# PReLU feed-forward over linear attention: four feature tiles of the first product by seven quarter products, and a computed order of loops 2 to 8

## The chip, the cores and the metric

The kernel runs on one core of a Trainium2 chip. The metric is the time of one execution on the device in microseconds (us), lower is better; runs of the unchanged kernel took 273.03, 273.45 and 273.68 us. The core has TensorE (PE, matmuls into PSUM), VectorE (DVE), ScalarE (ACT), GpSimd (POOL, here mostly for issuing DMAs) and SyncE (SP, for issuing DMAs). Each engine works through its own list of instructions in order, and semaphores tie the lists together.

## The reference

```
kv  = einsum('bhsd,bhse->bhde', k, v)           # batch 8, heads 8, seq 576, head_dim 64
o   = einsum('bhsd,bhde->bhse', q, kv)
o   = o / sqrt(mean(o*o, axis=-1) + 1e-6) * g_norm
x   = o.transpose(0,2,1,3).reshape(4608, 512)
h   = x @ w_in                                  # 512 -> 2048, the first product
g   = maximum(h, 0) + alpha * minimum(h, 0)
out = g @ w_out                                 # 2048 -> 512, the second product
```

## The kernel before

Matmul operands are float16, sums are float32 in PSUM. The 4608 tokens are cut into nine blocks of 512 (w = 0 to 8). x of a block lies transposed (feature rows, tokens along the free axis) in xt, two blocks at a time. The first product makes a block of h in sixteen tiles of 128 features by 512 tokens: m1_mm (L600) is four matmuls of 512 columns into one PSUM bank. m1_neg (L609, ScalarE) writes relu(-h) into m_sb, and m1_sum (L615, VectorE) makes g = h + (1 - alpha) * relu(-h) in float16 into gt.

The second product is already done with seven instead of eight products of quarters, from block 1 on (prod_mm, L796): a block of g is cut into halves of tokens and of features, w_out likewise; w_sum prepares sums of weight quarters once, s_sum (L731 to L737, VectorE) sums of g quarters, sixteen per block. Products 1 and 2 gather in PSUM bank X, 6, 7 and 4 in bank Y, 5 and 3 in bank Z, which is the same bank as Y. y_read takes the sums out: p1 and c11 by ScalarE copies (L824, L834), u2, u3, c21, c22, c12 by VectorE adds (L828, L838, L840) to parts read earlier. c11, c21, c22 are stored by GpSimd's queue and c12 by SP's.

Attention of block w + 1 runs inside loop w: row_kv (L1122) makes k'v of one batch, ScalarE copies it masked into kv_masked (L1134); rows_mm (L499) makes attention rows of two 128-token tiles at a time; rows_sq, rows_rs and rows_norm (L556 to L580) square, sum, take the reciprocal root and scale. A tile is squared either in eight 64-wide squares with an accumulator (L562) or, where 'red' is set, in one square and a VectorE reduction (L558); 'red' is set for one of four tiles in a steady loop. SP transposes the rows into xt (L585) and q into qt_sb (L380). Loads of k, v, q go out on GpSimd behind a small copy that waits for a given gt (gate), into two stage tiles per name (kst, vst, qst), two blocks ahead.

The order is written out by hand. Block 0 and the set-up stand before the loops; in loop w (1 to 8) each of sixteen units u emits one tile of the first product, then the sums listed for u (S_ALL, S_ONE, S_TWO, S_LST), then as many products of the second product as the lists X_AT and YZ_AT say (X of this block and Y, Z of the block before), then steps of attention (ROW_AT), transposes and loads. From block 2 on the tiles of the first product take turns in two PSUM banks (h1, h2), Y and Z in h0, X in a bank of its own, and attention has two pairs of banks (psr). After loop 8 the rest of block 8's second product follows.

## Time and profile before

| what | us |
|---|---|
| median of the runs | 273.45 (273.03 to 273.68) |
| span of the profiled execution, first to last instruction | 271.4 |
| median less that span | 2.05 |
| steady loop (block 3 to block 4, start of L631 to start of L631) | 27.59 |
| PE, DVE, ACT, POOL busy in that loop | 27.59, 23.27, 17.11, 11.33 |
| last loop; from its last tile to the end | 24.86; 13.86 |

The profile is of one execution; its own time beyond the span is not recorded apart, so the median of the runs stands beside it. A group's row gives the kernel's line, engine, operation, tile written and read, the shape, the count, the busy time with the mean of one, and the idle time ahead of it with what ended it. In a timeline a row gives the start, the time to the end of the last instruction merged into it, and the count. Durations of neighbours on an engine overlap, so the cost of one in a stream is the distance from its start to the next start.

### The profile page before, as it was taken

The page shows a single profiled execution, that of the slowest core. Times are in us where ns is not written, and L with a number is a line of the kernel's source. Part 1 is how long each engine was busy: PE and PEld are TensorE (multiplying, and loading weights), DVE is VectorE, ACT ScalarE, POOL GpSimd, SP SyncE. Part 2 cuts the span into 40 slices and gives each one's busy share as a digit, 9 for nine tenths or more (in the row PEclk, how much of TensorE's full clock was granted, in tenths as well). Part 3 has the DMA queues.
Part 4 walks back from the last instruction along what each step waited for, and adds up shares of the span by engine and source line. Part 5 has one row for each costly group of instructions (what it writes and reads, how often), then busy time and mean ns, then how long its engine had stood idle before and what let it go on. Part 6 is the DMA issues. An engine that isn't in the chain of part 4 may idle for free.

```text
span 271.4 us, 6175 instructions
## 1 busy us (share of the span) xinstructions
PE 265.4 (98%) x2286; PEld 168.8 (62%) x2286; DVE 216.9 (80%) x413; ACT 156.7 (58%) x532; POOL 87.5 (32%) x134
## 2 busy tenths in 40 slices
PE   7899999999999999999999999999999999999995
PEld 3354444456666666667666666666666666766684
DVE  6459657998959986998699869986998889878964
ACT  3467575786559447754776467546855864433410
POOL 8763462514551735163515351430110011101100
PEclk9999999999999999999999999999999999999999
DMA  7999999995999999969995999594061122211123
GB/s 155 195 202 203 195 198 194 160 212 101 157 129 243 159 165 140 170 105 177 135 159 105 174 121 156 131 151 102 19 138 40 41 47 88 62 40 40 40 77 118
DMA packets 91570, 35.58 MB, mean 131 GB/s; under 512 B 62980, under 2 KB 89748, under 8 KB 91540
## 3 DMA queue, kind: packets, MB, share of 16 engines
q0 software_dynamic: 57872, 23.83, 69.8%
q1 hardware_dynamic: 32628, 10.34, 22.8%
q10 hardware_dynamic: 1040, 1.02, 1.2%
q8 instruction: 18, 0.29, 0.4%
q14 instruction: 12, 0.10, 0.2%
HBM read 36.71 MB, written 9.44 MB: 170 GB/s over the span
## 4 chain that ended last, share of the span: by engine, by line
PE 81%; DMA 15%; POOL 2%; issue 1%; DVE 0%; POOLq 0%
PE h_ps L600 37%; PE yY L796 16%; PE yX L796 10%; PE yZ L796 10%; DMA w_out_sb<-in_moe_w_out_dram 5%; DMA vst<-in_v_dram 4%; DMA w_in_sb<-in_moe_w_in_dram 3%; DMA qst<-in_q_dram 2%; PE h_ps L631 2%; PE kv_ps L1122 2%; PE or_ps L499 2%; PE y L643 1%; PE yZ L791 1%; POOL w_in_sb L229 1%; PE kv_ps L418 0%
## 5 line engine op out<-in xcount | busy, mean ns | idle before, releaser
L600 PE MATMUL h_ps<-xt,w_in_sb 128*128 128x512 f16 x540 | 136.1, 379 | 0.0
L609 ACT ACTIVATE m_sb<-h_ps 128x512 f32<-128x512 f32 x144 | 86.6, 602 | 79.4 <-PE h_ps L600 59.9
L615 DVE SCALAR_TENSOR_TENSOR gt<-m_sb,beta_sb,h_ps 128x512 f16<-128x512 f32 x144 | 106.1, 743 | 23.1 <-ACT m_sb L609 20.5
L600 PEld LDWEIGHTS <-w_in_sb 128*128 128x128 f16 x540 | 51.4, 98 | 39.7 <-issue 0.4
L655 POOL DMA_DIRECT2D out_dram<-y_sb x32 | 20.5, 645 | 119.6 <-DVE y_sb L838 56.9
L796 PEld LDWEIGHTS <-s 128*128 128x128 f16 x496 | 48.3, 98 | 11.3 <-DVE s L733 0.3
L796 PEld LDWEIGHTS <-gt 128*128 128x128 f16 x384 | 37.5, 98 | 23.2 <-issue 0.2
L796 PE MATMUL yX<-w_out_sb,gt 128*128 128x256 f16 x256 | 44.6, 273 | 0.0
L796 PE MATMUL yY<-wsum,s 128*128 128x256 f16 x256 | 35.2, 273 | 0.0
L562 ACT ACTIVATE sq_sb<-or_ps 128x64 f16<-128x64 f32 x144 | 30.9, 256 | 2.3 <-PE or_ps L499 2.3
L562 ACT ACTIVATION_READ_ACCUMULATOR sq_sb<-or_ps 128x1 f32 x144 | 30.3, 242 | 0.0
L580 DVE TENSOR_TENSOR x_rows<-or_ps,rstd_r 128x512 f16<-128x512 f32 x27 | 18.4, 686 | 1.0 <-ACT rstd_r L572 1.0
L185 POOL DMA_DIRECT2D qst<-in_q_dram x20 | 17.7, 905 | 1.0 <-issue 1.0
L828 DVE TENSOR_TENSOR u<-yY,p 128x512 f32<-128x512 f32 x16 | 11.0, 690 | 8.2 <-PE yY L796 8.2
L796 PE MATMUL yY<-wsum,gt 128*128 128x256 f16 x128 | 17.6, 272 | 0.0
L796 PE MATMUL yZ<-wsum,s 128*128 128x256 f16 x120 | 17.5, 273 | 0.0
L796 PE MATMUL yZ<-w_out_sb,s 128*128 128x256 f16 x120 | 16.7, 273 | 0.0
L643 PE MATMUL y<-w_out_sb,gt 128*128 128x512 f16 x64 | 16.3, 379 | 0.3 <-DMA w_out_sb<-in_moe_w_out_dram 0.3
L731 DVE TENSOR_TENSOR s<-gt 128x512 f16<-128x512 f16 x32 | 13.3, 420 | 0.1
L733 DVE TENSOR_TENSOR s<-s,gt 128x512 f16<-128x512 f16 x32 | 12.8, 421 | 0.4
L737 DVE TENSOR_TENSOR s<-gt,s 128x512 f16<-128x512 f16 x32 | 12.7, 419 | 0.0
L735 DVE TENSOR_TENSOR s<-gt 128x512 f16<-128x512 f16 x32 | 12.3, 419 | 0.0
(107 smaller groups left out, 233.2 us busy)
## 6 DMA issues: line engine op xcount, KB each, us to landing
out_dram<-y_sb POOLq DMA_DIRECT2D x16, 256.0 KB, 2.8
kst<-in_k_dram POOLq DMA_DIRECT2D x7, 512.0 KB, 7.3
vst<-in_v_dram POOLq DMA_DIRECT2D x6, 512.0 KB, 8.0
qst<-in_q_dram POOLq DMA_DIRECT2D x20, 128.0 KB, 4.7
w_out_sb<-in_moe_w_out_dram POOLq DMA_DIRECT2D x8, 256.0 KB, 11.0
out_dram<-y_sb SPq DMA_DIRECT2D x5, 256.0 KB, 2.2
w_in_sb<-in_moe_w_in_dram POOLq DMA_DIRECT2D x2, 512.0 KB, 10.2
qst<-in_q_dram POOLq DMA_DIRECT2D x2, 512.0 KB, 12.1
```

The costliest lines, as they stand in the source:

```text
L185: nc.gpsimd.dma_start(out=st[:, t, :, :], in_=srcs["q"][b, :, t * P : (t + 1) * P, :].rearrange("h p d -> p h d"),)
L562: nc.scalar.activation(out=sq[:, half, j], in_=o_ps[:, half, j], func=AF.Square, accum_out=ssq[:, half, j : j + 1],)
L580: nc.vector.tensor_tensor(out=xr[:].rearrange("p j h d -> p h j d"), in0=o_ps, in1=rstd[:].unsqueeze(3).to_broadcast([P, 2, NPAIR, D]), op ...
L600: nc.tensor.matmul(out=h_ps[:], lhsT=w_in_blk(c, g), rhs=xts[w][:, c, :], start=(c == 0), stop=(c == NC - 1),)
L609: nc.scalar.activation(out=neg[w, g][:], in_=h_ps[:], func=AF.Relu, scale=-1.0)
L615: nc.vector.scalar_tensor_tensor(out=gts[w, i][:, r, :], in0=neg.pop((w, g))[:], scalar=beta_sb[:, g : g + 1], in1=h_ps[:], op0=ALU.mult, ...
L643: nc.tensor.matmul(out=y[:], lhsT=gt_cols(w, g, a * P, (a + 1) * P), rhs=w_out_blk(g), start=(n == 1), stop=(n == NF),)
L655: engs[store_turn[0] % len(engs)].dma_start(out=dst, in_=src)
L731: nc.vector.tensor_add(out=t[:], in0=a21, in1=a22)
L733: nc.vector.tensor_sub(out=t[:], in0=sums[w, 1, k][:], in1=a11)
L737: nc.vector.tensor_sub(out=t[:], in0=a12, in1=sums[w, 2, k][:])
L796: nc.tensor.matmul(out=bank, lhsT=lhs, rhs=rhs, start=fresh, stop=(c == NK - 1), skip_group_check=True,)
```

## The change

From block 3 on, the first product is done in two of its four feature groups (s = 2 and 3) by seven quarter products. A group is four feature tiles, 2s, 2s + 1 and 2s + 8, 2s + 9; its weights are cut into halves of features and of the contraction, x into halves of the contraction and of tokens. a_sum prepares four sums of weight quarters per group once, in stage tiles that are no longer used for loads; x_sum prepares four sums of x quarters per block. Products 1, 6, 7, 4 gather in one bank (Y) with ScalarE copies in between, the copy 'seed' also starts bank X for product 2, and 5 and 3 gather in bank V with VectorE adding u3 and u2 (c22, c12). Relu and PReLU sum follow per half, 256 wide, or, where 'asm' is set, 512 wide after one more copy.

In the second product bank Y is filled with p1 by a copy before product 6 (y_seed), so that u2, u3 and c21 are plain ScalarE copies. The feature order of all loops is F_ORDER, and the feature halves of the second product are LO and HI. From block 3 on k, v, q have one stage tile each. m_sb has four buffers in place of two, the first product four banks (h1, h2, m0, m1) in place of two, attention one pair of banks in place of two. In blocks 3 to 8 two tiles of a block are squared with the reduction in place of one, and one is normalised on ScalarE in eight pieces.

Loops 2 to 8 are no longer written out: each piece of work is a task with an engine, a cost in us, a due time and its dependencies; run_plan goes through time and gives each free engine the ready task that is due first; the instructions are emitted in that order.

```diff
+    M_BUFS = 4
...
+    def late_pools():
+        mid.close()
+        row_pool[:] = [
+            ctx.enter_context(tc.tile_pool(name="psr2", bufs=1, space=bass.MemoryType.PSUM))
+        ]
+        m_pool.append(
+            ctx.enter_context(tc.tile_pool(name="psm", bufs=1, space=bass.MemoryType.PSUM))
+        )
...
+    def stage_for(b, nm, shape):
+        if b < B_NAT:
+            return stage_tile(nm, shape)
+        if nm not in kept:
+            kept[nm] = stage_tile(nm, shape)
+        return kept[nm]
...
+    LO = (0, 4, 1, 5)
+    HI = (2, 6, 3, 7)
+    F_ORDER = [f for s in range(4) for f in (2 * s, 2 * s + 1, 2 * s + 8, 2 * s + 9)]
...
+    def s_sum(w, n, k, pool=0):
+        lo, hi = gts[w, LO[k]], gts[w, LO[k] if n == 3 else HI[k]]
...
+    def y_seed(w):
+        ybank[w, "Y"] = ps_h.tile([P, 2, HC], FP32, name="yY", tag="h0")
+        nc.scalar.copy(out=ybank[w, "Y"][:], in_=part[w, 1][:])
...
     def y_read(w, what, subs=(0, 1)):
+        seeded = 1 <= w < NW - 1
         if what == "p1":
             part[w, 1] = u_p.tile([P, 2, HC], FP32, name="p1")
             nc.scalar.copy(out=part[w, 1][:], in_=ybank[w, "X"][:])
             return
         if what in ("u2", "u3"):
             part[w, what] = u_p.tile([P, 2, HC], FP32, name=what)
+            if seeded:
+                nc.scalar.copy(out=part[w, what][:], in_=ybank[w, "Y"][:])
+                return
             nc.vector.tensor_add(
                 out=part[w, what][:], in0=ybank[w, "Y"][:], in1=part[w, 1][:]
             )
             return
         y_sb = ysb_p.tile([P, 2, HC], FP32, name="y_sb")
-        if what == "c11":
-            nc.scalar.copy(out=y_sb[:], in_=ybank[w, "X"][:])
+        if what == "c11" or what == "c21" and seeded:
+            nc.scalar.copy(out=y_sb[:], in_=ybank[w, what == "c11" and "X" or "Y"][:])
...
-    w_sum(3, 0)
+    w_sum(4, 1)
+    w_sum(3, 1)
...
+    M1_FROM = {2: 3, 3: 3}
...
+    def a_sum(s, n, pool=0):
+        if s not in spare:
+            spare[s] = stage_tile(SPARE[s], [P, 4, HD, 2 * P])
+        t = spare[s]
+        eng = nc.gpsimd if pool else nc.vector
+        sub, add = eng.tensor_sub, eng.tensor_add
+        if n == 1:
+            add(out=t[:, 0], in0=w_quad(1, s, 0), in1=w_quad(1, s, 1))
+        elif n == 2:
+            sub(out=t[:, 1], in0=t[:, 0], in1=w_quad(0, s, 0))
+        elif n == 3:
+            sub(out=t[:, 2], in0=w_quad(0, s, 0), in1=w_quad(1, s, 0))
+        else:
...
+    def x_sum(w, n, pool=0):
+        t = sum_p.tile([P, HD, HW], FP16, name=f"t{n}", tag=f"t{n}", bufs=1)
+        xsums[w, n] = t
+        sub = (nc.gpsimd if pool else nc.vector).tensor_sub
+        if n == 1:
+            sub(out=t[:], in0=x_quad(w, 0, 1), in1=x_quad(w, 0, 0))
+        elif n == 2:
+            sub(out=t[:], in0=x_quad(w, 1, 1), in1=xsums[w, 1][:])
+        elif n == 3:
+            sub(out=t[:], in0=x_quad(w, 1, 1), in1=x_quad(w, 0, 1))
+        else:
+            sub(out=t[:], in0=x_quad(w, 1, 0), in1=xsums[w, 2][:])
...
+    def m1_prod(w, s, n, bank, fresh):
+        t = m1s[w, s]
+        quad = {1: (0, s, 0), 2: (0, s, 1), 4: (1, s, 1)}.get(n)
+        lhs = w_quad(*quad) if quad else spare[s][:, {5: 0, 6: 1, 7: 2, 3: 3}[n]]
+        rhs = {1: (0, 0), 2: (1, 0), 3: (1, 1)}.get(n)
+        rhs = x_quad(w, *rhs) if rhs else xsums[w, {4: 4, 5: 1, 6: 2, 7: 3}[n]][:]
+        for c in range(HD):
+            for r in range(2):
+                nc.tensor.matmul(
+                    out=t[bank][:, r, :], lhsT=lhs[:, c, r * P : (r + 1) * P], rhs=rhs[:, c, :],
+                    start=(fresh and c == r == 0), stop=(c == HD - 1), skip_group_check=True,
+                )
+
+    def m1_fast(w, s, n, tags):
+        t = m1s.setdefault((w, s), {})
+        bank = {1: "Y", 6: "Y", 7: "Y", 4: "Y", 2: "X", 5: "V", 3: "V"}[n]
+        if n in (1, 5):
+            t[bank] = m1_bank(tags[bank], [P, 2, HW], f"m{bank}")
+        m1_prod(w, s, n, bank, n in (1, 5))
+
+    def m1_step(w, s, what, tags):
+        t = m1s[w, s]
+        if what == "seed":
+            t["X"] = m1_bank(tags["X"], [P, 2, HW], "mX")
+            nc.scalar.copy(out=t["X"][:], in_=t["Y"][:])
+        elif what in ("u2", "u3"):
+            t[what] = u_p.tile([P, 2, HW], FP32, name=f"m{what}")
+            nc.scalar.copy(out=t[what][:], in_=t["Y"][:])
+        elif what in ("c22", "c12"):
+            src, u = (t["V"], t["u3"]) if what == "c22" else (t["V"], t["u2"])
+            nc.vector.tensor_add(out=h_tile(t, what)[:, :, HW:W], in0=src[:], in1=u[:])
+        elif what in ("a11", "a21"):
+            src = t["X"] if what == "a11" else t["Y"]
+            nc.scalar.copy(out=h_tile(t, what)[:, :, 0:HW], in_=src[:])
+        elif what[1] in "AB":
...
+    def m1_out(w, i, r, cols, m, h):
+        if (w, i) not in gts:
+            gts[w, i] = gt_p.tile([P, 2, W], FP16, name="gt", tag=f"gt{i}")
+        g = 2 * i + r
+        nc.vector.scalar_tensor_tensor(
+            out=gts[w, i][:, r, cols], in0=m, scalar=beta_sb[:, g : g + 1], in1=h,
+            op0=ALU.mult, op1=ALU.add,
+        )
...
+    K = {"seed": -11.39, "u2": 5.39, "r11": -4.5, "s11": 12.84, "u3": -11.7, "c22": -13.97,
+        "r22": 24.44, "s22": 16.17, "c12": -43.75, "r21": 8.02, "s21": -21.99, "r12": 31.83,
+        "s12": 34.62, "f1": -61.14, "f5": -16.63, "f6": -44.59, "f2": -42.98, "f7": -46.9,
+        "f4": -54.78, "f3": 0.79, "r": 6.78, "s": 11.11, "S3": (27.56, 20.97, 19.62, -16.53),
+        "S1": (-26.68, -17.46, -58.31, 24.32), "S2": (-49.05, -13.6, 30.68, -11.23),
+        "S4": (66.79, 67.65, 50.06, 89.18),
+        "X": (60.08, 46.18, -72.53, 21.11, 34.85, 22.35, 44.64, 49.21), "yz0": -1.3, "yz": 1.22,
+        "rd": 68.4, "ysd": -7.18, "kv": -16.36, "row": (-5.77, 0.1), "rx": (31.6, 9.32),
+        "t": (15.09, 48.92, -16.97, 31.95), "ld": (3, 5, 12), "tail": (50.15,),
+        "a": (3.62, -3.21, -20.7, -8.13, 3.7, -30.12, -13.05, 8.8, -5.29, -7.6, -18.17, 6.66, 10.83, 19.05, 6.71, 19.29),
...
+        "asm": (1, 1, 1, 1, 0, 0, 0, 1), "red": (0, 1, 0, 1), "nact": (0, 1, 0, 0),
+        "slack": 1.04}
...
+            mm(1, K["f1"], *old("Y"), *xt_all)
+            mm(5, K["f5"], *old("V"), ("t", w, 1), ("a", s, 1))
+            step("seed", "ACT", "copy", K["seed"], key(1), *old("X"))
+            mm(6, K["f6"], key("seed"), key(1), ("t", w, 2), ("a", s, 2))
+            mm(2, K["f2"], key("seed"))
+            step("u2", "ACT", "copy", K["u2"], key(6), *prev("u2"))
+            mm(7, K["f7"], key("u2"), ("t", w, 3), ("a", s, 3))
+            step("u3", "ACT", "copy", K["u3"], key(7), *prev("u3"))
+            mm(4, K["f4"], key("u3"), ("t", w, 4))
+            step("c22", "DVE", "tt", K["c22"], key("u3"), key(5), ring="h")
+            mm(3, K["f3"], key("c22"), ("a", s, 4))
+            step("c12", "DVE", "tt", K["c12"], key(3), key("u2"), ring="h")
+            done = {}
+            for half, p1, p2, q, asm in (("A", "11", "12", 2, K["asm"][2 * s]), ("B", "21", "22", 4, K["asm"][2 * s + 1])):
+                old_gt = ("gt", w - 2, s + KQ * (half == "B"))
...
+            for n, what, eng, cost in ((6, "u2", "ACT", "copy"), (7, "u3", "ACT", "copy"),
+                                       (4, "c21", "ACT", "copy"), (5, "c22", "DVE", "tt"), (3, "c12", "DVE", "tt")):
+                for k in range(4):
+                    m = {6: 2, 7: 3, 5: 1, 3: 4}.get(n)
+                    need = (("S", w, m, k),) if m else hi(k)
+                    group(n, k, t1 + x * step, before, *need)
+                    before = ("p", w, n, k)
+                    x += 1
+                read(what, eng, cost, t1 + x * step - K["rd"], before, *((("y", w - 1, "c12"),) if what == "u2" else ()),
+                     *((("y", w - 1, "c22"),) if what == "u3" else ()))
...
+            task(("kv", w), "PE", "kv", t0 + K["kv"] * UNIT, lambda: kv_mm(w),
+                 (("ld", "k", w), ("ld", "v", w), *rows_free))
+            task(("kvc", w), "ACT", 0.76, t0 + K["kv"] * UNIT + 1.0, lambda: kv_copy(w), (("kv", w),))
...
+        b = w + 2
+        if b < B:
+            def go(nm, at):
+                f = F_ORDER[at - 1]
+                def fn():
+                    gate(gts[w, f // 2][0:1, f % 2, 0:1])
+                    load(nm, b)
+                deps = (*ready[w, f // 2], *((("kv", b - 1),) if nm != "q" else tuple(("q", b - 1, t) for t in range(NT))))
+                task(("ld", nm, b), "POOL", "loadq" if nm == "q" else "load", t0 + at * UNIT, fn, deps, lag=5.0 if nm == "q" else 7.5)
+            for nm, at in zip(("k", "v", "q"), K["ld"]):
+                go(nm, at)
+
...
+    def run_plan():
+        tasks.clear()
...
+        hs[:] = ["h1", "h2", "m0", "m1"]
+        for w in range(2, NW):
+            plan_m1(w)
+            plan_moves(w)
+            if w + 1 < NW:
+                plan_attention(w + 1)
+        for w in range(1, NW):
+            plan_m2(w)
+        plan_rest()
...
+                        if best is None or t["due"] < best["due"]:
+                            best = t
+                    if best is None:
+                        break
...
+    for t in run_plan():
+        t["fn"]()
+    w = NW - 1
+    LAST = [(3, i) for i in range(2 * NK)]
+    for n, i in LAST[:NK]:
```

## Prediction

> **What bounds the kernel now.** I read the page first, then the busy time of each engine loop by loop, then one steady loop in order of time on each engine, then the waits.
>
> The page's first line on TensorE, and the busy time of each engine in a steady loop (block 3 of the first product), in the last loop and in the tail:
>
> ```profile
> PE 265.4 (98%) x2286; PEld 168.8 (62%) x2286; DVE 216.9 (80%) x413; ACT 156.7 (58%) x532; POOL 87.5 (32%) x134
> ...
> core 0: us, PE busy (x) PEld busy (x) DVE busy (x) ACT busy (x) POOL busy (x), PEclk, DMA share, GB/s
> 95.37:122.96 27.59, 27.59 (x255) 18.50 (x252) 23.27 (x43) 17.11 (x74) 11.33 (x18) 1.00 1.21 145
> 232.68:257.54 24.86, 24.86 (x170) 16.18 (x168) 20.81 (x41) 9.95 (x18) 2.14 (x3) 1.00 0.13 44
> 257.54:271.40 13.86, 10.86 (x113) 9.52 (x111) 7.59 (x18) 1.18 (x2) 0.00 (x0) 1.00 0.28 96
> ```
>
> TensorE has no gap in a loop: 27.59 of 27.59 us at granted clock 1.00. VectorE has 4.3 us to spare, ScalarE 10.5. In the tail 10.86 us of matmuls are followed by 3.0 us in which the last stores land. A busy row does not say how densely matmuls stream, so I take start to start from the timeline:
>
> ```profile
> 121.33 1.03 PE L600 MATMUL h_ps<-xt,w_in_sb 128*128 128x512 f16 x4
> 122.19 0.93 PE L796 MATMUL yX<-w_out_sb,gt 128*128 128x256 f16 x7
> ...
> 264.72 1.91 PE L796 MATMUL yY<-wsum,gt 128*128 128x256 f16 x16
> 266.47 1.04 PE L796 MATMUL yZ<-w_out_sb,s 128*128 128x256 f16 x8
> ```
>
> Four 512-column matmuls take 0.86 us (0.215 each), sixteen 256-column ones 1.75 us (0.109 each). Every span of TensorE is streaming, so only fewer columns make it shorter. VectorE and ScalarE in the same way, where they are not idle:
>
> ```profile
> 111.77 0.69 DVE L838 TENSOR_TENSOR y_sb<-yY,p 128x512 f32<-128x512 f32 x1
> 112.37 0.74 DVE L615 SCALAR_TENSOR_TENSOR gt<-m_sb,beta_sb,h_ps 128x512 f16<-128x512 f32 x1
> 113.03 0.69 DVE L580 TENSOR_TENSOR x_rows<-or_ps,rstd_r 128x512 f16<-128x512 f32 x1
> 113.63 0.74 DVE L615 SCALAR_TENSOR_TENSOR gt<-m_sb,beta_sb,h_ps 128x512 f16<-128x512 f32 x1
> 114.28 0.42 DVE L737 TENSOR_TENSOR s<-gt,s 128x512 f16<-128x512 f16 x1
> 114.62 0.69 DVE L580 TENSOR_TENSOR x_rows<-or_ps,rstd_r 128x512 f16<-128x512 f32 x1
> ...
> 97.85 0.60 ACT L609 ACTIVATE m_sb<-h_ps 128x512 f32<-128x512 f32 x1 [0.27 <-PE h_ps L600]
> 98.35 0.58 ACT L834 COPY y_sb<-yX 128x512 f32<-128x512 f32 x1
> ```
>
> So one VectorE add out of PSUM costs 0.60 us, one PReLU sum (L615) 0.66, one float16 sum 0.34; a ScalarE relu costs 0.50, and a copy 0.46 (the p copy of L824 starts at 115.08, the next square at 115.54). Who waits for whom:
>
> ```profile
> ACT m_sb L609 <- PE h_ps L600: 59.9, 80, 1.2
> DVE gt L615 <- ACT m_sb L609: 20.5, 32, 1.4
> DVE u L828 <- PE yY L796: 8.2, 11, 1.5
> ```
>
> The other engines wait for TensorE, not the reverse.
>
> **The change, part by part.**
>
> *Seven quarter products (m1_prod, m1_fast), two groups in each of loops 3 to 8.* A group is four feature tiles: before, 16 matmuls of 512 columns, 16 x 0.215 = 3.44 us; after, 7 x 4 of 256 columns, 28 x 0.109 = 3.06. That is 0.38 a group, 0.76 a loop, and 12 groups give 4.6 us, all on the path, since TensorE has no idle time there. A steady loop would be 26.83.
>
> The Trainium skill has a rule that speaks against this. "TensorE: Matmul & The Clock Gate", section "Back-to-back issue gap", gives sustained spacings of about 81 ns at 128 columns and 131 ns at 512; between them I estimate some 98 ns at 256, and a group would then go from 2.1 to 2.7 us, a loss of some 7.7 us over twelve. The trace does not bear that out: its 512-column matmuls start 215 ns apart, and by them the 4.6 us stand, so it gets no chance of its own.
>
> *VectorE.* Out go, per loop, three adds of the second product (u2, u3, c21) and one normalisation: 4 x 0.60 = 2.40. In come two c adds per group, 4 x 0.60 = 2.40; four x_sum, 4 x 0.34 = 1.36; one more reduction (L558, 0.59 from 110.78 to 111.37); and in three of the four halves of the groups the L615 sums run 256 wide. The trace has a 256-wide sum of this kind at L476 (480 ns against 745), so 0.66 - 0.27 = 0.39 each, and a half costs 4 x 0.39 - 2 x 0.66 = 0.24 more, three of them 0.7. Net +2.65: 25.9 busy in a loop of 26.83. This was hidden with 4.3 us to spare and now has 0.9. The eight a_sum (8 x 0.34 = 2.7) fall once, around loops 2 and 3, and loop 2 has no groups and 4.3 us of room: 0.
>
> *ScalarE.* In come four copies for the second product and three per group, 10 x 0.46 = 4.6; one asm copy 0.46; one full-width square 0.49; one normalisation in eight 64-wide pieces. For such a piece the nearest row is the 64-wide square (L562), 0.10 alone and 0.20 with its accumulator read, so 0.8 to 1.6; I take the upper end, the row that also ends in a second step. Out go eight square pairs, 8 x 0.20 = 1.6. Net +5.55: 22.7 of 26.83. Hidden, if in time.
>
> *New handoffs (m1_step, y_seed).* Within a group products 1, 6, 7, 4 share one bank, and between them ScalarE must copy (seed, u2, u3) before TensorE may go on; product 3 waits for VectorE's c22. That is 4 a group and one new seed in the second product: 9 a loop. One costs TensorE up to some 0.9 us (a copy of 0.58 and the wake-ups on both sides; the single waits of ScalarE for L600 run up to 1.2), and nothing where other matmuls stand between. So 0 to 8 us a loop. The nearest row is the four such handoffs per loop that the second product has now (u2, u3, c21, c22): they leave TensorE idle 0.0 in the loops. But that cover was an L600 tile after each few products; half of these tiles are gone, and VectorE's room has shrunk to 0.9. I take a third of one handoff, 0.3 us a loop: 1.8 over six loops, and 0.2 for loop 2, 2.0 in all. Behind a handoff that is late, everything on TensorE's queue waits, and so do the relus behind it.
>
> *Single stage buffers for k, v, q from block 3; loads moved.* The load of block b+1 must now follow kv of block b. Loads are issued at nearly the same places as before (gate, two DMAs: 0.2 + 0.7 + 0.9 on GpSimd); landing took 6.1 to 9.6 us for k and v, against a next use one attention step later. kv may be ordered on TensorE right behind the landing; its wait could then be 0 to the 3.5 us of spread in each of four blocks, 0 to 14. The nearest row, kv_ps of L1122, waited 0.2 us in all for vst: I take 0. On GpSimd's queue a load behind a store that waits for c21 or c22 would come later by that wait (5.3 and 4.2 us in the steady loops); the room of some 12 us from landing at about 115 to kv at 127.8 covers it. SP keeps nine transposes a loop, landing 2.4 to 6.1 us after issue: 0.
>
> *Feature order, w_sum moves, reads of c11 to c22, LAST order.* The same instructions at other places; the tail's 10.9 us of matmuls and 3.0 us of stores stay: 0.
>
> Sum: 271.4 - 4.6 + 2.0 = 268.8 of span. The median of the runs shown, 273.45, is 2.05 above the profiled span of 271.4 (the runs go from 1.7 to 2.3 above); with the same around it, 270.9.
>
> **Rivals.**
>
> *VectorE becomes the bound (slower).* Place: loops 3 to 8. 25.9 us busy plus whatever idle time its own waits leave. Today that is 4.3 us a loop, 2.6 of it for ScalarE's m_sb. It decides from 1.7 us on: 25.9 + 1.7 is the loop of before. If half of today's idle time stays, 2.15, a loop takes 28.05, +0.46, six are +2.8: 276.2. If all of the 2.6 stays, 28.5 and 279. For: 97% busy and a fixed order. Against: today's waits come from TensorE being slow to deliver, and two more m_sb buffers and two more PSUM banks come with the change.
>
> *The handoffs are exposed (slower).* If two of nine a loop show in full, 1.8 us against 0.76: +1.04 x 6 = +6.2, 279.7. For: three of the four banks are one group's. Against: the second product's 112 matmuls a loop (12.2 us) are free to fill.
>
> *The gain is eaten (no change).* Stalls of 0.76 a loop, 0.9 of a handoff: 273.5.
>
> *The clock gives way.* The first ten warm-up matmuls start 0.44 us apart, twice the 0.216 of later ones:
>
> ```profile
> 1.46 4.45 PE L297 MATMUL warm_ps<-y_sb 128*128 128x512 f16 x10 [1.46 <-DVE y_sb L119]
> ```
>
> If gaps brought that state back for as long (4.4 us at half rate) once in each of six loops, that is 6 x 2.2 = 13 us: 284. Against it: gaps of 0.27 to 0.36 us at 7 to 12 us did not bring it back. The Trainium skill, "TensorE: Matmul & The Clock Gate", section "A second HAM failure mode: psum-queue depth-cycling", reports a kernel whose small idles between matmul groups did just this; no run here shows it in the loops.
>
> **How the numbers follow.** Gain kept in part, as summed: 0.60, own range 268.4 (no stall, 0.4 for the uncertain offset) to 272.6 (stalls of 0.6 a loop). Eaten: 0.08, within 0.2% (0.55 us, about what runs that scatter by 0.65 can tell). VectorE 0.20, handoffs 0.10, clock 0.02, all slower. Prediction 270.9. The range goes from 268.4 to 277.0: it leaves out a third of the VectorE case, most of the handoff case, the clock and a few hundredths below, some 0.19. Faster 0.60, same 0.08, slower 0.32.
>
> **What would show it.** Right: steady loops of about 27.1 us from block 3 on, some 540 - 192 = 348 full-width matmuls of L600's kind, 336 quarter ones 0.109 apart, TensorE idle some 0.3 us a loop, VectorE about 96% busy. Wrong: TensorE waiting for VectorE's gt or s in every loop (VectorE the bound), for u2, u3 or seed copies (handoffs), for vst or kst (single buffers), or matmuls twice as far apart (clock).

## The result and the profile after

The changed kernel takes 283.0 us (median; 282.4 to 284.4), the one before takes 273.56 beside it on the same chip. The ratio is 1.035, with a 95% interval of 1.031 to 1.039: slower by 9.4 us, where 270.9 was forecast and the range ended at 277.0. The profiled execution took 284.4 us, span 282.6.

The page of the changed kernel: span, busy time of each engine, the granted clock in forty slices, and the shares of the chain that ended last.

```profile
span 282.6 us, 6544 instructions
...
PE 266.1 (94%) x2430; PEld 184.8 (65%) x2430; DVE 229.6 (81%) x484; ACT 194.8 (69%) x560; POOL 87.5 (31%) x134
...
PEclk9999999999999999999979999689999999999999
...
PE 61%; DMA 23%; DVE 8%; ACT 2%; POOL 2%; issue 2%; SPq 1%; DVEq 0%; POOLq 0%
```

TensorE's busy time is 0.7 us above that of before (265.4), though it has fewer columns to stream, and its idle time is 282.6 - 266.1 = 16.5 us against 271.4 - 265.4 = 6.0. Together that is +11.2, the whole difference of the spans. The clock row has two dents, and transfers hold 23% of the chain that ended last (15% before).

The loops of the changed kernel, from the first matmul of L675 of a block to that of the next (blocks 3 to 6), with the columns as in the table of the prediction:

```profile
95.59:122.46 26.87, 25.99 (x264) 19.76 (x265) 19.73 (x42) 21.10 (x79) 7.61 (x12) 1.00 1.11 131
122.46:155.55 33.09, 28.66 (x282) 21.46 (x280) 25.63 (x54) 24.45 (x83) 14.16 (x22) 0.95 1.26 129
155.55:185.00 29.45, 26.32 (x250) 19.45 (x248) 23.48 (x50) 20.37 (x62) 9.67 (x15) 0.89 1.19 136
185.00:212.88 27.88, 27.88 (x257) 21.60 (x256) 24.61 (x51) 22.81 (x89) 2.51 (x4) 0.99 0.34 88
```

The loop of block 3 takes 26.87 us, shorter than the 27.59 of before. The loops of blocks 4 and 5 take 33.09 and 29.45, and in both the clock is below 1. TensorE's longest waits (line, what it waits for: us in total, times, longest), and its timeline at each of them:

```profile
PE or_ps L522 <- DMA qt_sb<-qst: 4.3, 1, 4.3
PE kv_ps L1314 <- DMA vst<-in_v_dram: 3.1, 1, 3.1
PE h_ps L675 <- DMA xt<-x_rows: 1.9, 2, 1.1
...
PE yY L868 <- DVE s L802: 0.4, 1, 0.4
```

```profile
141.25 0.82 PE L522 MATMUL or_ps<-kv_masked,qt_sb 64*128 64x64 f16 x24 [4.33 <-DMA qt_sb<-qst]
142.00 1.03 PE L868 MATMUL yY<-wsum,s 128*128 128x256 f16 x4
142.83 1.06 PE L1225 MATMUL mY<-t,w_in_sb 128*128 128x256 f16 x4
...
145.47 1.04 PE L868 MATMUL yX<-w_out_sb,gt 128*128 128x256 f16 x8
...
179.75 0.43 PE L1314 MATMUL kv_ps<-vst,kst 128*64 128x64 f16 x8 [3.13 <-DMA vst<-in_v_dram]
179.96 0.27 PE L1314 MATMUL kv_ps<-vsb,ksb 128*64 128x64 f16 x2
180.01 0.43 PE L1314 MATMUL kv_ps<-vst,kst 128*64 128x64 f16 x8
```

The four long waits are all for transfers, and VectorE and ScalarE hold TensorE up by no more than 0.4 us in the loops. Behind the wait of 4.33 us four matmuls of 256 columns take 0.83 to 0.85 us (start to start, 142.00 to 142.83 to 143.68), later ones 0.44: the clock is at half rate. The trace's clock record has 1.00 except from 141.24 to 144.65 and from 178.78 to 185.61, 3.41 and 6.83 us, each at one of these two waits.

The account against before, in us: waits 4.33 + 3.13 + 1.87 + 0.4 = +9.8; half rate +4.6 (10.24 us, less 0.97 of it still spent waiting, of which half is lost); fewer columns -4.6; idle time ahead of block 2, 3.57 up to 68.33 in place of 3.02 up to 67.00, +0.5. That is +10.3 of the 11.2; 0.9 has no row of its own.

Why the transfers are late: the summary of a tile ends with the time from issue to landing (minimum, median, maximum). For v (vst, issues from 100 to 185 us) before and after:

```profile
L176 POOL DMA_DIRECT2D vst<-in_v_dram x3: 885/890/892, 106.6 to 161.9; - x3
...
DMA to landing us min/median/max: 6.1/7.4/7.8
```

```profile
L200 POOL DMA_DIRECT2D vst<-in_v_dram x3: 885/885/892, 106.9 to 166.3; - x3
...
DMA to landing us min/median/max: 8.9/11.7/13.3
```

and for the five transposes of q of batch 6 in the changed kernel (issues from 122 to 150 us), with GpSimd's timeline beside them:

```profile
L403 SPq DMA_TRANSPOSE qt_sb<-qst x4: 1199/1252/1849, 130.6 to 135.6; - x4
...
DMA to landing us min/median/max: 3.9/8.8/9.7
```

```profile
131.49 0.91 POOL L200 DMA_DIRECT2D kst<-in_k_dram  x1
133.43 0.89 POOL L200 DMA_DIRECT2D vst<-in_v_dram  x1
```

The transposes (130.6 to 137.0) and the loads of k and v of batch 6 are in flight together. Before the change the same five transposes of q were issued from 124.1 to 129.8, and k and v from 130.0 on:

```profile
L380 SPq DMA_TRANSPOSE qt_sb<-qst x4: 1198/1211/1231, 124.1 to 128.1; - x4
...
DMA to landing us min/median/max: 3.4/6.1/6.1
```

The time that a load has until it is needed shrank as well. Before the change, v of batch 5 was issued at 106.56 and first read at 127.83, 21.3 us later, and for batches 6 and 7 it was 21.3 and 21.2. In the changed kernel v of batch 7 is issued at 166.34 and TensorE comes to it at 179.75 - 3.13 = 176.62, 10.3 us later (10.6 and 16.1 for batches 5 and 6); it lands after 13.3.

The reason stands in the code of the change: the planner credits a load of k or v with a landing time of 7.5 us, a transpose of q or x with 3.4, and lets the matmuls that read them come right behind that. So the theory is: **(T) late transfers.** Loads and transposes collide, the order has no slack for it, and TensorE's wait lowers the clock for some microseconds more. The rivals: **(R1)** the clock gives way by itself, without long waits; **(R2)** the seven products with their handoffs, or VectorE, cost the time, and the waits are only where it shows; **(R3)** the single stage buffers force the loads to be late.

### The profile page after: what moved, and what is told of

Same layout as the page of the kernel before. It is cut to its first block, busy times and chain, and to the rows that moved or that the text cites. A ratio compares the mean times of both kernels' runs of the same rounds, so it can differ in the third digit from the quotient of the medians.

```text
span 282.6 us, 6544 instructions
## 1 busy us (share of the span) xinstructions
PE 266.1 (94%) x2430; PEld 184.8 (65%) x2430; DVE 229.6 (81%) x484; ACT 194.8 (69%) x560; POOL 87.5 (31%) x134
## 4 chain that ended last, share of the span: by engine, by line
PE 61%; DMA 23%; DVE 8%; ACT 2%; POOL 2%; issue 2%; SPq 1%; DVEq 0%; POOLq 0%
PE h_ps L643 17%; PE yY L868 13%; DMA vst<-in_v_dram 11%; PE yZ L868 7%; PE yX L868 7%; PE mY L1225 6%; DMA kst<-in_k_dram 5%; DMA xt<-x_rows 5%; DMA qt_sb<-qst 3%; PE mV L1225 3%; PE y L687 3%; PE or_ps L522 2%; DVE gt L1292 2%; DVE gt L658 1%; PE mX L1225 1%
## 5 line engine op out<-in xcount | busy, mean ns | idle before, releaser
L643 PE MATMUL h_ps<-xt,w_in_sb 128*128 128x512 f16 x348 | 82.7, 379 | 0.0
L658 DVE SCALAR_TENSOR_TENSOR gt<-m_sb,beta_sb,h_ps 128x512 f16<-128x512 f32 x96 | 68.3, 740 | 6.3 <-ACT m_sb L652 5.3
L652 ACT ACTIVATE m_sb<-h_ps 128x512 f32<-128x512 f32 x96 | 56.5, 608 | 19.9 <-PE h_ps L643 13.7
L643 PEld LDWEIGHTS <-w_in_sb 128*128 128x128 f16 x348 | 33.3, 98 | 32.3 <-issue 0.2
L868 PE MATMUL yX<-w_out_sb,gt 128*128 128x256 f16 x256 | 34.5, 273 | 0.0
L1292 DVE SCALAR_TENSOR_TENSOR gt<-m_sb,beta_sb,mh 128x256 f16<-128x256 f32 (+1 forms) x48 | 24.0, 543 | 0.5 <-ACT m_sb L1285 0.5
L585 ACT ACTIVATE sq_sb<-or_ps 128x64 f16<-128x64 f32 x96 | 20.6, 253 | 5.1 <-PE or_ps L522 5.1
L585 ACT ACTIVATION_READ_ACCUMULATOR sq_sb<-or_ps 128x1 f32 x96 | 20.2, 238 | 0.0
L1285 ACT ACTIVATE m_sb<-mh 128x512 f32<-128x512 f32 x30 | 18.7, 634 | 2.0 <-DVE mh L1247 1.6
L1244 ACT COPY mu<-mY 128x512 f32<-128x512 f32 x24 | 14.2, 590 | 8.2 <-PE mY L1225 8.1
L1247 DVE TENSOR_TENSOR mh<-mV,mu 128x512 f32<-128x512 f32 x24 | 16.5, 686 | 2.7 <-PE mV L1225 2.2
```

What stands on the lines that cost most here:

```text
L585: nc.scalar.activation(out=sq[:, half, j], in_=o_ps[:, half, j], func=AF.Square, accum_out=ssq[:, half, j : j + 1],)
L643: nc.tensor.matmul(out=h_ps[:], lhsT=w_in_blk(c, g), rhs=xts[w][:, c, :], start=(c == 0), stop=(c == NC - 1),)
L652: nc.scalar.activation(out=neg[w, g][:], in_=h_ps[:], func=AF.Relu, scale=-1.0)
L658: nc.vector.scalar_tensor_tensor(out=gts[w, i][:, r, :], in0=neg.pop((w, g))[:], scalar=beta_sb[:, g : g + 1], in1=h_ps[:], op0=ALU.mult, ...
L868: nc.tensor.matmul(out=bank, lhsT=lhs, rhs=rhs, start=fresh, stop=(c == NK - 1), skip_group_check=True,)
L1247: nc.vector.tensor_add(out=h_tile(t, what)[:, :, HW:W], in0=src[:], in1=u[:])
```

## The experiments

**Matmuls in the two waits (e1_busy, and e1_look for its trace).** Twenty matmuls of 512 columns ahead of the second row step of block 5, fifteen ahead of kv of batch 7, each into the bank that the step overwrites:

```diff
     def rows_mm(w, tiles):
         o_ps = row_tile([2, 2, NPAIR, D], "or_ps")
+        if (w, tiles[0]) == (5, 3):
+            fill(o_ps[:, 0], 20)
...
+        if b == 7:
+            both = row_tile([2, 2, NPAIR, D], "kv_ps")
+            fill(both[:, 1], 15)
+            kv_ps = kv_tiles[b] = both[:, 0, 0]
```

> The changed kernel with one addition: 20 matmuls of 512 columns on constants ahead of the second row step of block 5, and 15 ahead of kv of batch 7, into PSUM that the step overwrites; so TensorE streams while it would stand still. Theory A (two late transfers hold TensorE for 4.3 and 3.1 us, and each wait then costs as much again because the clock falls to half): the transfers stay late, the waits shrink to what 4.3 and 3.2 us of filling leave, the granted clock is 1.00 throughout, and of the 283.0 us some 5 go, 278. Theory B (VectorE or ScalarE full, the waits are where their backlog shows): the clock may stay up, but the time moves by less than 1.5 us, since the matmuls are not the bound. Theory C (the clock falls for another reason than these waits): it falls again at other places, 283.

> The kernel of e1_busy once more for its trace (its time was 280.25 us, 2.8 less than the changed kernel, 5 were expected). Theory A: the two filled places hold no half-rate stretch any more; the 3.4 us at half rate that the mean clock of 0.994 still holds stand behind another wait of TensorE, and the two late transfers cost what the filling doesn't cover. Theory C: the half-rate stretch stands where TensorE had no wait of a microsecond or more in the 4 us before.

Measured: 280.25 us, ratio to before 1.024 (1.021 to 1.028); 2.8 us went where 5 were expected. In the execution of e1_look the time was 280.1, span 278.3, and the clock record shows 1.00 from the warm-up to the last stores. TensorE's timeline there:

```profile
136.73 4.48 PE L512 MATMUL or_ps<-w_in_sb,mask 128*128 128x512 f16 x20
141.14 0.52 PE L532 MATMUL or_ps<-kv_masked,qt_sb 64*128 64x64 f16 x24
...
174.77 3.40 PE L512 MATMUL kv_ps<-w_in_sb,mask 128*128 128x512 f16 x15
178.10 0.32 PE L1329 MATMUL kv_ps<-vst,kst 128*64 128x64 f16 x8
178.25 0.20 PE L1329 MATMUL kv_ps<-vsb,ksb 128*64 128x64 f16 x2
```

The row step comes at 141.14 as it came at 141.25: the transfers are as late as before (q transposes up to 10.0 us, v 13.1), and work that nobody needs costs nothing while they are awaited. But its 24 matmuls are followed 0.46 us later by the next, not 0.75, and the span is 4.3 us shorter than that of the change. The medians differ by only 2.8: in other executions of the change the mean clock was 0.988 and not 0.982, so one stretch of 3.41 us at half rate fewer.

In the profiled execution of e1_busy itself (281.25 us) the mean clock was 0.994: it has one such stretch, from 8.04 to 11.46, in the set-up, and 1.00 from there on. Ahead of it stand two short waits:

```profile
6.03 0.45 PE L359 MATMUL qt_ps<-ident,mu 96*64 96x96 f16 x12 [0.69 <-DVE mu L982]
...
8.01 0.53 PE L426 MATMUL kv_ps<-vst,mu 96*64 96x64 f16 x12 [0.83 <-DMA vst<-in_v_dram]
```

So right behind the warm-up the clock did fall without a long wait, which is what the third theory of the expectation had as its sign. In the loops it did not: both places that were at half rate in the change are at full rate once TensorE is kept busy there. There the half rate comes from the idle time, and R1 falls for the loops. This half rate is worth 2.8 us by the medians and 4.3 by the spans, beside the 4.6 of the account. The rest of the loss is the time waited.

**No loads of k and v for batch 6 (e2_noload6, and e2_look for its trace).** The products of batch 6 are computed from what the stage tiles still hold, so the output differs from the reference in that batch:

```diff
-                    load(nm, b)
+                    if b == 6 and nm != "q":
+                        stages[b, nm] = kept[nm]
+                    else:
+                        load(nm, b)
```

> The changed kernel, same order, without the loads of k and v of batch 6 (1.1 MB; batch 6 is computed from what the stage tiles hold, batch 3 to 5). These loads run beside the q transposes of block 5. Theory A with collision of transfers: the q transposes land within 5 us in place of 8.8, the 4.3 us wait of the second row step and the first half-rate stretch (3.4 us, worth 1.7) go, 283.0 - 6.0 = 277; the wait for v of batch 7 and the second half-rate stretch stay. Theory A with slow transposes of their own: landing stays near 8.8, and the time near 283. Theory B: time within 1.5 us of 283, another wait takes the place.

> The kernel of e2_noload6 once more for its trace (274.63 us, 8.4 less than the changed kernel, 6.0 were expected). Theory A with collision: the q transposes of block 5 land within 5 us, the second row step of block 5 has no wait, and v of batch 7 comes with less of a wait too, since what follows runs at other times; at most one half-rate stretch of 3.4 us is left. Theory A with slow transposes of their own: they land near 8.8 us, and the gain comes from elsewhere.

Measured: 274.63 us (272.64 to 277.31), 1.003 (0.9995 to 1.006); 277 was expected. In the execution of e2_look the span was 271.6 with a clock of 1.00. The transposes of q of batch 6, by the same summary as above:

```profile
L403 SPq DMA_TRANSPOSE qt_sb<-qst x4: 1197/1208/1538, 130.2 to 134.9; - x4
...
DMA to landing us min/median/max: 2.3/2.4/2.6
```

With two loads of 512 KB gone they land in 2.4 us, not 8.8, and the row step waits for nothing. v of batch 7 is waited for 0.8 us in place of 3.1, and the loop of block 4 takes 26.97 in place of 33.09. The span falls by 11.0; the waits that went and the half rate sum to 4.33 + 2.3 + 4.6 = 11.2. Not every execution does as well: in the profiled one of e2_noload6 (span 274.6) v of batch 7 is waited for 2.2 us, and a wait of 2.4 for x of block 3 is followed by 3.41 us of half rate. There too the transposes of q land in 2.3 to 2.6. The collision that T names is shown: two transfers fewer take away nearly the whole loss, 8.4 of 9.4 us by the medians. The seven products and their handoffs are all still there, so R2 can hold only what is left of the better span to 271.4 - 4.6 = 266.8: 4.8 us, of which 3.0 are waits for x and v.

**The two steps later in the order (e4_later).** The second row step of block 5 goes back by 4.4 us, kv of batch 7 by 3.2, and with them what depends on them (moved adds that to the planned start and sorts again):

```diff
-    for t in run_plan():
+    for t in moved(run_plan(), {("R", 5, 3): 4.4, ("kv", 7): 3.2}):
         t["fn"]()
```

> The changed kernel with two steps moved back in the order: the second row step of block 5 by 4.4 us and kv of batch 7 by 3.2 us, and what depends on them as far as it must; nothing else. Theory A: both waits fall below 1 us, the clock stays at 1.00, and 7.4 + 5.1 us go: 270.5, if the attention steps behind them have room; where they have none, the wait comes back at the next tile of the first product, with 273 to 278. Theory B: the time stays within 1.5 us of 283.

Measured: 278.26 us, 1.017 (1.015 to 1.019), at the upper end of the 273 to 278 expected where the attention steps have no room. In its timeline the wait for q is gone and another has come:

```profile
147.21 0.43 PE L1314 MATMUL kv_ps<-vst,kst 128*64 128x64 f16 x8 [2.93 <-DVE x_rows L611]
147.41 0.27 PE L1314 MATMUL kv_ps<-vsb,ksb 128*64 128x64 f16 x2
```

The change left attention one pair of PSUM banks. kv of the next batch needs it, and must now wait until VectorE has normalised the rows that were made later. Part of the loss is gone, the rest is handed to the next step of the attention chain, with half rate from 146.90 to 150.31 again. A later reader has no room in this order, so the order as a whole must change, or the transfers.

**The loads of batches 6 and 7 earlier (e6_early).** Without their gate, right behind the load of q, 6 to 8 us sooner (k and v of batch 6 at 125.47 and 127.02 in place of 131.49 and 133.43, of batch 7 at 156.18 and 158.81 in place of 164.60 and 166.34):

```diff
-                    gate(gts[w, f // 2][0:1, f % 2, 0:1])
+                    if b < 6 or nm == "q":
+                        gate(gts[w, f // 2][0:1, f % 2, 0:1])
                     load(nm, b)
...
+    for t in moved(order, {("ld", "k", 6): 54.6, ("ld", "v", 6): 56.6, ("ld", "k", 7): 79.4, ("ld", "v", 7): 81.4}):
```

> The changed kernel with four DMA pairs moved forward on GpSimd's queue and their gate copies left out: k and v of batch 6 right behind q of batch 5, k and v of batch 7 right behind q of batch 6, some 7 to 9 us earlier than before; TensorE, VectorE and ScalarE keep their order. Theory A (late landing, kv and row steps right behind it): v of batch 7 and the q transposes of block 5 no longer run beside each other, both waits of TensorE (4.3 and 3.1 us) fall below 1 us, the clock stays at 1.00, and of 283.0 some 7 to 12 us go, 271 to 276. If the loads only meet other transposes (those of x, or q of batch 5), a wait of 1 to 3 us appears there. Theory B (VectorE and ScalarE full): the time stays within 1.5 us of 283.

Measured: 287.84 us, 1.053 (1.047 to 1.059). A miss by 12 us, to the other side: slower than the change. TensorE's waits:

```profile
PE or_ps L522 <- DMA qt_sb<-qst: 10.4, 2, 5.7
PE h_ps L675 <- DMA xt<-x_rows: 1.7, 2, 1.0
...
PE kv_ps L1314 <- DMA vst<-in_v_dram: 0.8, 1, 0.8
```

The wait for v shrank to 0.8 as meant, but the loads now run beside the q transposes of two batches, where they ran beside those of one, and TensorE waits 4.6 and 5.7 us. That the loads could go out 6 to 8 us sooner, with the same single buffers, speaks against R3: v of batch 7 had its stage tile free from the end of kv of batch 6 (about 150.3) and was issued at 166.34 because the order put it there. What counts is beside what a load runs, not only when it starts.

**Without the seven products (e3_plain, and e3_look for its trace).** All sixteen tiles by plain matmuls, same planner, same due times:

```diff
-    M1_FROM = {2: 3, 3: 3}
+    M1_FROM = {}
...
```

> The changed kernel without the seven products in the first product (all sixteen tiles plain in every loop, no weight or x sums), same scheduler, same numbers, so another order comes out. TensorE has 4.6 us more to do. Theory A: its time depends on where its own order puts kv and the row steps; the loss belongs to the scheduler's order, and with waits for transfers of 5 to 10 us the time is 278 to 290; VectorE has some 31 us less to do over the loops, and this doesn't help. Theory B: with VectorE and ScalarE relieved the waits go, 273 to 275. Theory D (the seven products themselves cost more than 16 plain matmuls): 273 or less.

> e3_plain once more for its trace: no group of the first product by seven products, the rest of the change kept; it took 291.45. If the loss sits in the order alone, a loop without a wait takes 27.6 us as before the change (the 0.76 us of fewer columns missing), and the waits for the transposed q and for v of batches 6 and 7 are there, together 7 us or more, with half rate behind them; the span is then 282.6 + 4.6 = 287 or some more. If the seven products themselves cost time (handoffs, VectorE), the waits on transfers are there but the undisturbed loops are not longer than 26.9.

Measured: 291.45 us, 1.068 (1.061 to 1.075), above the 278 to 290 expected; in the execution of e3_look 291.1, span 289.3. TensorE's waits there:

```profile
PE h_ps L675 <- DMA xt<-x_rows: 4.0, 1, 4.0
PE kv_ps L1314 <- DMA vst<-in_v_dram: 2.7, 1, 2.7
...
PE yX L868 <- ACT p L904: 1.3, 2, 0.7
PE yY L868 <- ACT yY L895: 1.2, 1, 1.2
PE yX L868 <- ACT y_sb L917: 1.2, 2, 1.0
PE h_ps L643 <- DVE gt L658: 0.9, 1, 0.9
```

As an undoing of one part this is not clean: removing the products moves all the rest, the waits sit at other places (x of block 3 and v, not q as expected), and 10.24 us of half rate follow them. It shows that the loss does not need the seven products, and that the products are not what made the kernel slow. Their worth can't be read from it, since 4.6 us of waits for copies and for gt came in as well.

**The order computed anew with landing times from the trace (e5_retimed).** The landing times that the planner credits are raised, the due times (K) and the choices of engine were searched again for the shortest plan; the work that it orders is that of the change, apart from those choices:

```diff
-                task(("ld", nm, b), "POOL", "loadq" if nm == "q" else "load", t0 + at * UNIT, fn, deps, lag=5.0 if nm == "q" else 7.5)
+                task(("ld", nm, b), "POOL", "loadq" if nm == "q" else "load", t0 + at * UNIT, fn, deps, lag=6 if nm == "q" else 12.5)
-            task(("q", b, t), "SP", "turn", t0 + at * UNIT, lambda b=b, t=t: dma_t(b, (t,)), deps, lag=3.4)
+            task(("q", b, t), "SP", "turn", t0 + at * UNIT, lambda b=b, t=t: dma_t(b, (t,)), deps, lag=8)
-                task(("x", w, i), "SP", "turn", d + 1.4, lambda i=i: x_move(w, i), (("n", w, i),), lag=3.4)
+                task(("x", w, i), "SP", "turn", d + 1.4, lambda i=i: x_move(w, i), (("n", w, i),), lag=6.5)
...
-        "asm": (1, 1, 1, 1, 0, 0, 0, 1), "red": (0, 1, 0, 1), "nact": (0, 1, 0, 0),
...
+    K = {'seed': -305.82, ... 'asm': (0, 0, 0, 1, 0, 1, 1, 1), 'red': (0, 1, 1, 1), 'nact': (0, 0, 0, 0), 'slack': 1.04}
...
```

> The changed kernel with the same instructions, but the order computed with landing times as the changed kernel's trace shows them in their late cases: 12.5 us for k and v, 8 for q transposes, 6.5 for x transposes, 6 for q (before: 7.5, 3.4, 3.4, 5), and with due times chosen anew for these. Theory A: no wait of TensorE for a transfer above 1 us, clock 1.00; the span is the one of before less 4.6 plus some 1 to 3 us of short gaps, 269 to 272 us of time, which beats both kernels. Theory B: the side engines hold the loops whatever the transfers do, 277 or more.

Measured: 271.65 us (270.25 to 274.54), 0.995 of before (0.992 to 0.998): 11 us below the change, 1.4 below the kernel before. One wait for a transfer is left in its loops:

```profile
103.93 0.59 PE L675 MATMUL h_ps<-xt,w_in_sb 128*128 128x128 f16 x4 [2.04 <-DMA xt<-x_rows]
```

with half rate from 103.91 to 107.32 behind it in the profiled execution (274.1 us, clock 0.994; the other nine had 0.998 to 1.00). T explains the loss, and the change has a gain, of 0.5%, once the order is right. The run changes two things at once, the landing times, and the due times and choices of engine found in a new search. A new search with the old landing times was not run, so how much of the 11 us each of them is worth is not shown. The single buffers are kept here, and no wait for k or v is left in the loops, which speaks against R3 once more.

**Once more, with a longer landing for x of block 3 (e7_best).** The due times were searched again, and the asm choices with them, so four of the eight differ; against e5_retimed:

```diff
-                task(("x", w, i), "SP", "turn", d + 1.4, lambda i=i: x_move(w, i), (("n", w, i),), lag=6.5)
+                task(("x", w, i), "SP", "turn", d + 1.4, lambda i=i: x_move(w, i), (("n", w, i),), lag=10.5 if w == 3 else 7.5)
...
```

> Same instructions as e5_retimed, order computed once more with the landing times of the trace (12.5 us for k and v, 8 for the q transposes, 6 for q, 10.5 for the x transposes of block 3 and 7.5 for the others), since the one wait left in e5_retimed was 2.04 us for the x transposes of block 3, with 1.7 us of half rate behind it. If late transfers and the clock behind them were the whole loss, TensorE has no wait over 1 us left in the loops, the clock stays at 1.00, and the 4.6 us of fewer columns come through: 273.1 - 4.6 + up to 1.5 of small stalls = 268.5 to 270. If the handoffs between the seven products or VectorE ate part of the gain, the time stays at 271 to 272 with waits of TensorE for mu, mh or gt; if another transfer becomes the late one, 272 to 275 with a wait named for it.

Measured: 271.89 us, 0.996 (0.994 to 0.999), where 268.5 to 270 was expected. The waits are as T expects, the time is not. All of TensorE's waits above 0.5 us, and four loops:

```profile
PE warm_ps L320 <- DVE y_sb L131: 1.5, 1, 1.5
PE yZ L868 <- ACT y_sb L917: 0.9, 1, 0.9
PE yY L868 <- ACT u L909: 0.7, 1, 0.7
PE qt_ps L359 <- DVE mu L972: 0.6, 1, 0.6
```

```profile
123.69:151.67 27.98, 27.98 (x326) 21.55 (x324) 27.00 (x55) 22.98 (x61) 11.34 (x17) 1.00 1.52 161
151.67:178.24 26.57, 26.57 (x274) 20.44 (x272) 26.28 (x56) 20.04 (x53) 10.02 (x15) 1.00 1.29 142
178.24:202.77 24.53, 24.53 (x242) 18.66 (x240) 24.26 (x50) 20.67 (x69) 1.42 (x2) 1.00 0.50 95
202.77:226.29 23.52, 23.52 (x202) 18.03 (x200) 23.04 (x47) 17.85 (x35) 1.42 (x2) 1.00 0.21 47
```

No wait for a transfer in the loops, the clock at 1.00, and a span of 269.9 against 271.4. TensorE is busy for 261.3 us, 4.1 less than before the change: nearly all of the 4.6. Its idle time is 8.6 against 6.0: 1.6 in two handoffs of the second product around block 2 (the copies of L917 and L909), 0.8 ahead of the loops (3.85 idle up to 68.38, against 3.02 up to 67.00), 0.1 in the tail. So -4.1 + 2.5 = -1.6, and the measured spans differ by 1.5. What keeps the time above 270 are handoffs, as R2 has it, 1.6 us of them, the start, and 0.5 of the fewer columns that did not come. VectorE is busy for 100.6 of these four loops' 102.6 us, 98%, and TensorE still has no gap in them.

## Why the prediction was wrong

*The step that failed* is "Single stage buffers for k, v, q from block 3; loads moved": its bounds were 0 to 14 us, and it took 0 from a row of the kernel before, where kv waited 0.2 us for vst. That row was made by an order in which v had 21.3 us from issue to use, and the change replaces that order. The row that would have told is in the code: the planner's landing times of 7.5 and 3.4 us against landings of 6.1 to 9.6 and 2.4 to 6.1 that the prediction itself quotes. An order packed to such a margin waits whenever a landing is longer. For v even the quoted 9.6 would have fitted into the 10.3 us that batch 7 had; it took the 13.3 of the new order. Measured: 3.1 us for v, 4.3 for q and 1.9 for x, and 4.6 of half rate behind the first two. The end of 14 was named, and then not taken into the range.

*"SP keeps nine transposes a loop, landing 2.4 to 6.1 us after issue: 0"* failed with it. That k and v now go out beside the q transposes was not asked. These took 8.8 us (median) beside k and v, 2.4 without them (e2_look), and 6.1 before the change. The landing of v itself went from 7.4 to 11.7 (medians); its cause alone was not tried.

*The buffers themselves* were not the cause: in the change the tile was free long before the load (150.3 against 166.34), e6_early issues the loads earlier with the same tiles, and e7_best has no wait for k or v with them. The gate and the order set the time of issue.

*The seven products*: -4.6 on TensorE was right to within 0.5: e7_best has 4.1 us less of TensorE, and 348 full-width matmuls of L643 are left as forecast. That the loop of block 3 took 26.87, close to the 26.83 worked out without stalls, is luck: 0.9 of it is idle and 25.99 busy, since the planner moves work from one loop to another.

*VectorE and ScalarE*: 25.9 and 22.7 us a loop were forecast; blocks 3 to 7 of the change have 19.7 to 26.3 and 20.4 to 24.5. VectorE did not become the bound, and its rival (0.20) did not come in, not even at the 98% of e7_best.

*The handoffs*: 2.0 us were put down. The change shows 0.4 (a wait for s in block 2), e7_best 1.6. The size was fair, the place was not (block 2 and not the steady loops), and the rival of 0.10 did not come in.

*The clock* had 0.02 and a time of 284, close to what came, by luck and for another reason: it was given six small losses behind handoffs and got two behind waits for transfers. They explain 4.6 of the loss and not 13. In the loops of all the traces at hand no drop came behind a wait under 2 us; in the set-up of e1_busy one came behind 0.69 and 0.83.

## What to carry to other kernels

When a change replaces the order of the work, a row that says "no wait here" says nothing of the new order: take the landing time that the new order counts on, set it against the longest landing in the trace, and ask which other transfers will be in flight. Count a wait of TensorE of 2 us or more with the half rate that may follow it: 2.04 us of waiting in e5_retimed brought 3.41 us of it, 1.7 more. Fed with landing times as they are under load, and with its due times searched anew, the planner brought the same change from 283.0 to 271.7 us.

## What the runs showed of the hardware

**The clock changes on a fixed grid.** In the trace of the change the stretches at full clock between warm-up and the first drop, and between the two drops, last 136.53 and 34.13 us: 40 and 10 times 3.413. In e6_early they are 136.53 and 23.89 (40 and 7 times), in e5_retimed 98.99 (29 times), in e4_later 139.95 (41 times), in e3_look 92.16 and 44.37 (27 and 13 times). With the grid known, each wait of TensorE can be laid over its windows:

| run | wait, us | idle in the window before a drop could come, of 3.41 | clock |
|---|---|---|---|
| the change, q | 4.33 | 3.41 | half for 3.41 |
| the change, v | 3.13 | 2.16, then 0.97 | half for 6.83 |
| e6_early, q | 4.64 | 3.12 | half for 3.41 |
| e6_early, q | 5.72 | 3.41, then 2.19 | half for 6.83 |
| e3_look, x | 3.97 | 2.89, then 1.08 | half for 6.83 |
| e3_look, v | 2.73 | 2.11, then 0.62 | half for 3.41 |
| e4_later, norm | 2.93 | 2.62, then 0.31 | half for 3.41 |
| e5_retimed, x | 2.04 | 2.02 | half for 3.41 |
| e1_look, x | 2.70 | 0.94, then 1.76 | full |
| e3_plain, x | 4.65 | 2.58, then 2.07 | half for 6.83 |
| e3_plain, v | 2.82 | 1.62, then 1.20 | full |
| e2_noload6, x | 2.38 | 2.19 | half for 3.41 |
| e2_noload6, v | 2.17 | 0.70, then 1.48 | full |
| e1_busy, set-up | 0.69 and 0.83 | 1.52 | half for 3.41 |

In the loops a window with 2.02 us or more idle was followed by half rate, one with 1.76 or less was not, and a wait of 2.70 that fell across two windows cost only itself. The window of e1_busy, the first one at full clock behind the warm-up, does not fit: 1.52 us idle were enough there, and no run shows why. At half rate, 0.97 us idle kept the clock down for another window and 0.62 did not. That these are thresholds is read from the waits of this table, not tried on purpose.

The Trainium skill, "TensorE: Matmul & The Clock Gate", section "What's actually happening", describes a free-running window of 3413 ns; the grid of these traces agrees with it. The same page of the Trainium skill, section "Why this matters for your kernels", asks for no idle gap above about 3 us; the wait of 2.04 us in e5_retimed dropped the clock all the same, so here that advice is not strict enough.

**Loads slow transposes by DMA.** Five transposes of q landed in 2.3 to 2.6 us without the loads of k and v of that batch, and in 3.9 to 9.7 beside them, two of 512 KB each; before the change, in another order, in 3.4 to 6.1. The other direction, v landing in up to 13.3 us in the change with transposes of x issued from 0.7 us behind it, against 7.8 before, stands in the traces but was not tried alone.
